# Attention beside a mixer MLP on one core: nine of sixteen key blocks in two 16-bit parts, and VectorE's background work in two classes

## The chip, the core and the metric

The kernel runs on one core of a Trainium2 chip. TensorE multiplies matrices into PSUM, VectorE and ScalarE do elementwise work, GpSimd fills constants and starts a few transfers, and SyncE's queue starts most of the DMA transfers. Each engine works through its own instructions in order and meets the others through semaphores. The metric is device time in microseconds of one execution.

## The reference

With x of 2048 tokens by 640 channels, 32 heads of 20 channels, and 1536 hidden channels of the MLP:

```python
xn = _layernorm(x, axis=-1)
return x + _A_ref(xn, A_wqkv, A_wo) + _B_ref(xn, B_w1, B_b1, B_w2, B_b2)
# _A_ref(x, wqkv, wo): q, k, v of 32 heads from x @ wqkv
scores = jnp.einsum("bhqd,bhkd->bhqk", q, k) * (Dh ** -0.5)
p = _softmax(scores, axis=-1)
o = jnp.einsum("bhqk,bhkd->bhqd", p, v)      # then @ wo
# _B_ref: normalises once more, then
h = _gelu(jnp.einsum("bsd,df->bsf", y, w1) + b1)
return jnp.einsum("bsf,fd->bsd", h, w2) + b2
```

All of it is float32. The kernel reaches that with products of 16-bit parts (a high part and a remainder), or with TensorE's slower float32 products.

## The kernel before

**Up to about 240 us** x is normalised and transposed, q, k and v are computed, and the weights of the MLP are split into 16-bit parts. The values v stay in SBUF, one block of rows per 128 keys. `SPLIT` (L25) says in which form: for a split block (two of every four) as a high and a low float16 part, for a whole block as float32. `vproj_out` (L355) writes them; VectorE computes the low part of a split block (L361).

**The attention stage** runs from there to about 1310 us. It has 64 passes, each for a pair of heads `g`, half of the tokens `hf`, and 512 tokens of that half `cc`. A pass goes over 16 key blocks in four groups of four (`GRP`). For each key block `scores` (L578) multiplies keys by queries for both heads on TensorE (L584) and ScalarE takes the exponential (L586) into a tile `p` of 128 keys by 2 heads by 512 tokens, float32. There are seven tiles `p` and three PSUM slots for scores. The sums over the keys are taken in `pv` (L603), one group behind: when the scores of a group are all issued, `pv(prev)` multiplies the group before. Its output is one PSUM tile `o` of 128 rows in four quarters of 32 rows. Each product (L615) has 32 output rows and so takes a quarter of TensorE's columns. A head has two quarters: 0 and 1 for the first, 2 and 3 for the second; `opart` receives both, and they are added later.

- For a split block, the upper 16 bits of `p`, read as bfloat16, are multiplied by the high value part in one quarter and by the low value part in the other: four products of 512 tokens for two heads. The remainder `low = p - upper(p)` in float16, which `rest` (L593) computes on VectorE (L598), is multiplied by the high value part: one product per head, alternating between the head's quarters from block to block.
- For a whole block, `p` and the values are multiplied in float32, one product per head, again alternating between the quarters.

`low` has four buffers. `rest` is called for the first block of a group after the second block's scores, and for the others after the fourth block's, just ahead of `pv(prev)`.

**The fill.** Between these, TensorE is given the MLP: `layer1` (L777) and `layer2` (L811), in portions with costs, and after them the output projection (L872). In each group, after the second block's scores, a credit grows by `rate` = 1.235 us, and portions are drawn while there is credit (L943 to L951). Both use the single PSUM bank pool `psM`, so the next tile of products waits until VectorE has read the one before: `gelu` (L735) for `layer1`, `addup` (L755) for `layer2`.

**The background work** is a list of Python generators, `sides`, each of which issues some instructions and yields. `tick` (L526), called after every second key block, takes one step of every generator in the list:

```python
def tick():
    for it in list(sides):
        if next(it, self_end) is self_end:
            sides.remove(it)
```

In that list are: `gelu` (seven VectorE instructions and a tanh on ScalarE, over five steps), `addup`, the loads of keys and queries (`load_stack`), the preparation of the output weights (`prep_late`, L534), and `finishing` (L661). The last normalises heads that are done: `finish` (L666) loads the two partial sums of some heads and the sums of exponentials, takes reciprocals (L702 to L707), sends them out and loads them back spread over rows, and then does four VectorE instructions on each strip of 512 tokens: add, multiply, high part, remainder (L725 to L731). A strip ends in a store to `oscr`, which the projection reads. `UNITS` gives the pairs of heads taken together; there are 23 strips.

At the end, after the last pass, the projection runs from `oscr` on its own (some 70 us), with the last heads' normalisation beside it.

Of the kernel before, what the change touches and what calls it, by code (L numbers as in the profile page):

```python
# [12 lines left out]
ALU = mybir.AluOpType  # L13
# [8 lines left out]
VW = DH + 1  # L22
PAD = 32 - VW
VROW = H * VW + PAD
SPLIT = (1, 1, 0, 0) * (NKB // 4)  # L25
NPAIR = H // 2
EPS = 1e-5
TOP = 15.5
# [7 lines left out]
TAIL = 12  # L36
# [6 lines left out]
def mha_mlp_kernel(tc, x, wqkv, wo, w1, b1, w2, b2, out):  # L43
# [4 lines left out]
    with (  # L48
# [463 lines left out]
        with ExitStack() as scope:  # L512
# [4 lines left out]
            ptp = pool(name="pt", bufs=2 * GRP - 1)  # L517


            sides = []  # L520

            def begin(it):

                if next(it, self_end) is not self_end:
                    sides.append(it)

            def tick():
                for it in list(sides):
                    if next(it, self_end) is self_end:
                        sides.remove(it)  # L530

            self_end = object()

            def prep_late(tag, w, wv_, src, nk, slices, delay):  # L534
                nc.sync.dma_start(w, src)
                for _ in range(delay):
                    yield
                acc = sm.tile([P, 8], F32, tag="acc", name="acc")
                for i, sl in enumerate(slices):
                    junk = m1.tile([P, 2 * MC], F32, tag="u", name="junk").bitcast(BF16)[:, :D]  # L540
                    nc.scalar.activation(junk, w[:, sl, :], AF.Square, accum_out=acc[:, i : i + 1])
                    yield
                pw[tag] = pow2(acc[:, : len(slices)], tag)
                s = keep.tile([P, 1], F32, name=f"s_{tag}")
                nc.vector.tensor_scalar(s, pw[tag][1], 4096.0, None, ALU.mult)
                nc.vector.tensor_scalar(fo, pw["v"][0], 2.0**-22, pw[tag][0], ALU.mult, ALU.mult)
                yield
                for k in range(nk):
                    parts = []
                    for tag_, c0 in (("u", 0), ("w", 320)):  # L550
                        tmp = m1.tile([P, 2 * MC], F32, tag=tag_, name="wtmp")[:, :320]
                        nc.vector.tensor_scalar(tmp, w[:, k, c0 : c0 + 320], s, None, ALU.mult)
                        parts.append((tmp, slice(c0, c0 + 320)))
                    yield
                    for tmp, cols in parts:
                        nc.vector.tensor_copy(wv_[:, k, 0, cols], tmp)
                        nc.vector.tensor_sub(wv_[:, k, 1, cols], tmp, wv_[:, k, 0, cols])
                    yield

            def project(ot, acc, t0, j):  # L560
                for hf in range(2):
# [41 lines left out]
            def pv(units):  # L603

                g, hf, cc, kb0 = units[0][:4]
                if kb0 == 0:
                    pv.o = psO.tile([P, 512], F32, tag="o", name="o")  # L610
                    pv.begun = set()
                last = units[-1][3] == NKB - 1

                def product(q, src, v0, t):
                    nc.tensor.matmul(pv.o[32 * q : 32 * q + 32, :], src[:, v0 - PAD * (1 - q % 2) :][:, :32], t,  # L615
                                     start=q not in pv.begun, stop=last, skip_group_check=True)
                    pv.begun.add(q)

                split = [(u[3], upper(u[4]), u[5]) for u in units if SPLIT[u[3]]]
                whole = [(u[3], u[4]) for u in units if not SPLIT[u[3]]]  # L620
                of16 = lambda kb, a: 2 * PAD + kb * 2 * VROW + (2 * g + a) * 2 * VW
                of32 = lambda kb, a: PAD + kb * VROW + (2 * g + a) * VW
                for kb, up, _ in split:
                    for a in range(2):
                        product(2 * a, vhalf, of16(kb, a), up[:, a])
                        product(2 * a + 1, vhalf, of16(kb, a) + VW, up[:, a])
                for a in range(2):
                    for n, (kb, _, low) in enumerate(split):
                        product(2 * a + n % 2, vhalf, of16(kb, a), low[:, a])
                for a in range(2):  # L630
                    for n, (kb, pt) in enumerate(whole):
                        product(2 * a + n % 2, vfull, of32(kb, a), pt[:, a])
                if last:
                    if cc == 0:
                        evs[g, hf] = m1.tile([P, 2, 512], F32, tag="ev", name="ev")
                    nc.scalar.activation(evs[g, hf][:, cc], pv.o, AF.Copy)  # L636
                    if cc == 1:
                        unload(g, hf, evs.pop((g, hf)))
# [5 lines left out]
            def unload(g, hf, ev):  # L644
                cols = slice(hf * 1024, (hf + 1) * 1024)
                for p in range(2):
                    dma(g, hf)(lpart[p, hf, 2 * g : 2 * g + 2, :].rearrange("a (c t) -> a c t", c=2),
                                      ev[PAD + DH + VW * p :: 64])
                    for a in range(2):
                        q0, r = 64 * a + PAD + VW * p, (2 * g + a) * DH  # L650
                        dma(g, hf)(opart[p, r : r + DH, cols].rearrange("d (c t) -> d c t", c=2),
                                          ev[q0 : q0 + DH])
                if g + 1 in ENDS:
                    fins.append(finish(g + 1 - UNITS[ENDS.index(g + 1)], g + 1, hf))
                    if len(fins) == 1:
                        sides.append(finishing())

            fins = []
            ready = [0, 0]
# [6 lines left out]
            def finish(g0, g1, hf):  # L666
# [9 lines left out]
                for c0 in range(0, 1024, w):  # L676
# [21 lines left out]
                    if c0 == 0:  # L698
                        for _ in range(W1 if last else 4):
# [3 lines left out]

                        nc.vector.tensor_scalar(l[:, 1], l[:, 0], LO, None, ALU.is_ge, ALU.min,
                                                accum_out=good[: nh * 16, n : n + 1])
                        nc.vector.tensor_scalar(l[:, 0], l[:, 0], 1e-30, None, ALU.max)
                        nc.vector.reciprocal(l[:, 1], l[:, 0])  # L707
                        if not last:
# [26 lines left out]
            def gelu(ps, r2f, hT, f):  # L735
                u = m1.tile([P, 2, MC], F32, tag="u", name="u")
                w = m1.tile([P, 2, MC], F32, tag="w", name="w")
                if f == 0:
                    nc.vector.tensor_scalar(r2f, r2f, f1, None, ALU.mult)
                nc.vector.tensor_mul(u, ps, r2f[:, None, :].to_broadcast([P, 2, MC]))  # L740
                nc.vector.tensor_add(u, u, b1t[:, f : f + 2, None].to_broadcast([P, 2, MC]))  # L741
                yield

                nc.vector.tensor_mul(w, u, u)  # L744
                nc.vector.scalar_tensor_tensor(w, w, 1.0 / 0.044715, u, ALU.add, ALU.mult)  # L745
                yield
                yield
                nc.scalar.activation(w, w, AF.Tanh, scale=0.7978845608028654 * 0.044715)
                yield
# [1 line left out]
                nc.vector.tensor_scalar(hT[:, f : f + 2, 0, :], u, ch, None, ALU.mult)  # L751
                nc.vector.scalar_tensor_tensor(hT[:, f : f + 2, 1, :], u, ch, hT[:, f : f + 2, 0, :],  # L752
                                               ALU.mult, ALU.subtract)

            def addup(ps, xb, t0, hf):  # L755
                cols = slice(hf * 320, (hf + 1) * 320)
                nc.vector.scalar_tensor_tensor(xb[:, cols], ps[:, :320], f2, xb[:, cols], ALU.mult, ALU.add)  # L757
                if hf == 1:
                    yield
                    nc.sync.dma_start(accscr[t0 : t0 + P, :], xb)  # L760
                    if t0 + P < S:
                        load_xb(t0 + P)
# [1 line left out]
            NMC = S // MC  # L764

            xs, hTs = {}, {}
            over = [False]

            def load_chunk(mc):
# [3 lines left out]
                nc.sync.dma_start(xnt, xscr[:, :, :, t0 : t0 + MC])  # L773
                nc.sync.dma_start(r2f, rscr[None, t0 : t0 + MC].to_broadcast([P, MC]))
                xs[mc] = xnt, r2f

            def layer1(mc, f):  # L777
                xnt, r2f = xs[mc]
# [91 lines left out]
            W1, W2 = 24, 17  # L870

            def projection():  # L872
                known = lambda c: ready[2 * c // NMC] == len(UNITS)
                for c in range(NMC):
                    while not known(c):
                        yield None
# [50 lines left out]
            with tc.manual_schedule():  # L927
# [2 lines left out]
                rate = 1.235  # L930
                groups = [(g, hf, cc, kb) for g, hf in ORDER for cc in range(2) for kb in range(0, NKB, GRP)]
                prev = None
                for g, hf, cc, kb0 in groups:
                    units = []
                    for kb in range(kb0, kb0 + GRP):
# [4 lines left out]
                        if kb % GRP == 1:  # L940
# [2 lines left out]

                            rest(units[0])
                            credit += rate
                            spent, over[0] = 0.0, False
                            while credit > 0 and spent < CHUNK and not over[0]:
                                cost = next(fill)
                                if cost is None:
                                    credit = 0.0  # L950
                                    break  # L951
                                credit -= cost
                                spent += cost
                        else:
                            for u in units[1:]:
                                rest(u)
                            if prev:
                                pv(prev)
                    prev = units
                    if cc == 0 and kb0 == 0 and (g, hf) != ORDER[-1]:  # L960
                        n = ORDER[ORDER.index((g, hf)) + 1]
# [16 lines left out]
                pv(prev)  # L978
                while more(1):
                    pass  # L980
                while sides:
                    tick()
                flag = nc.values_load(badi, min_val=0, max_val=1)
        with tc.If(flag > 0):
# [98 lines left out]
```

## Time and profile before

| | |
|---|---|
| median of 3 runs | 1384.71 us (1384.6 to 1388.05) |
| profiled execution | 1385.2 us, span 1383.5 us |
| TensorE products busy | 1350.8 us, 98% of the span |
| ScalarE busy | 1126.2 us, 81%; exponentials 973.6 us, x1024 |
| VectorE busy | 1061.7 us, 77%; `low` 608.8 us, x512 |
| gelu on VectorE | 7 instructions of 0.49 to 0.75 us, x48 |
| strips of head normalisation on VectorE | 4 instructions of 0.43 to 0.71 us, x23 |
| granted TensorE clock | 0.997 |
| HBM traffic | 123.7 MB, 89 GB/s over the span |

A row of the groups gives line, engine, operation, output and inputs, shapes and count, then busy time and mean duration of one, then the idle time of the engine just before these instructions and what ended it. TensorE's instructions overlap, four quarters above all, so their mean durations are longer than the distance from one to the next. In a row of stretches, each engine's busy time stands with its number of instructions; the last numbers are the granted clock, the busy share of the DMA engines and GB/s. A row of waits says who waited for whom, for how long in all, how often, and the longest.

### The profile page before, as it was taken

The page shows a single profiled execution, that of the slowest core. Times are in us where ns is not written, and L with a number is a line of the kernel's source. Part 1 is how long each engine was busy: PE and PEld are TensorE (multiplying, and loading weights), DVE is VectorE, ACT ScalarE, POOL GpSimd, SP SyncE. Part 2 cuts the span into 40 slices and gives each one's busy share as a digit, 9 for nine tenths or more (in the row PEclk, how much of TensorE's full clock was granted, in tenths as well). Part 3 has the DMA queues.
Part 4 walks back from the last instruction along what each step waited for, and adds up shares of the span by engine and source line. Part 5 has one row for each costly group of instructions (what it writes and reads, how often), then busy time and mean ns, then how long its engine had stood idle before and what let it go on. Part 6 is the DMA issues. An engine that isn't in the chain of part 4 may idle for free.

```text
span 1383.5 us, 29113 instructions
## 1 busy us (share of the span) xinstructions
PE 1350.8 (98%) x11711; PEld 600.9 (43%) x11711; DVE 1061.7 (77%) x1425; ACT 1126.2 (81%) x1282; POOL 32.9 (2%) x75
## 2 busy tenths in 40 slices
PE   9999999999999999999999999999999999999998
PEld 6555555443333343433343333343334334333375
DVE  6648743899778977889887789877988897888642
ACT  5644323999999999999999999999999999999700
POOL 2000000000000000000000000000000000000000
PEclk9999999999999999999999999999999999999999
DMA  9853413012124231213221123212124322341375
GB/s 265 243 175 109 108 52 110 16 32 64 41 55 111 67 88 34 69 52 102 71 77 33 47 75 103 76 47 58 44 64 113 98 56 70 85 153 59 98 235 179
DMA packets 92320, 125.68 MB, mean 91 GB/s; under 512 B 16905, under 2 KB 58569, under 8 KB 92178
## 3 DMA queue, kind: packets, MB, share of 16 engines
q1 hardware_dynamic: 89218, 117.14, 28.3%
q0 software_dynamic: 2304, 5.24, 2.3%
q8 instruction: 94, 1.54, 0.5%
q10 hardware_dynamic: 656, 1.36, 0.3%
q14 instruction: 48, 0.39, 0.1%
HBM read 80.84 MB, written 42.86 MB: 89 GB/s over the span
## 4 chain that ended last, share of the span: by engine, by line
PE 59%; DVE 11%; ACT 5%; DMA 3%; issue 2%; SPq 1%; DVEq 0%; ACTq 0%
PE o L615 23%; PE s L584 14%; PE py L819 9%; PE pu L787 8%; DVE low L598 5%; PE z L896 5%; ACT p L586 4%; DMA oscr<-oa 1%; DVE u L740 1%; DMA oa<-opart 1%; DVE u L741 1%; DVE w L744 1%; DVE w L745 1%; DVE hT L752 1%; DVE u L750 1%
## 5 line engine op out<-in xcount | busy, mean ns | idle before, releaser
L586 ACT ACTIVATE p<-s 128x1024 f32<-128x1024 f32 x1024 | 973.6, 1042 | 52.4 <-PE s L584 46.2
L598 DVE TENSOR_TENSOR low<-p 128x1024 f16<-128x1024 f32 x512 | 608.8, 1219 | 165.0 <-ACT p L586 164.9
L615 PE MATMUL o<-p,vfull 128*32 128x512 bf16 (+1 forms) x4096 | 433.7, 494 | 0.0
L584 PE MATMUL s<-qs,ks 61*128 61x512 f16 x2048 | 317.7, 382 | 8.7 <-ACT p L586 7.2
L584 PEld LDWEIGHTS <-ks 61*128 61x128 f16 x2048 | 63.9, 94 | 296.4 <-issue 294.2
L787 PE MATMUL pu<-xm,w1t 128*128 128x256 f16 x1440 | 179.2, 274 | 4.1 <-DVE u L740 3.6
L819 PE MATMUL py<-w2t,hT 128*128 128x320 f16 x1152 | 178.6, 301 | 1.7 <-DVE xb L757 1.7
L787 PEld LDWEIGHTS <-w1t 128*128 128x128 f16 x1440 | 130.9, 98 | 71.2 <-issue 57.6
L819 PEld LDWEIGHTS <-hT 128*128 128x128 f16 x1152 | 102.5, 98 | 89.5 <-issue 55.2
L286 PE MATMUL qkp<-xnt,wv 128*128 128x512 f16 x600 | 132.3, 380 | 0.0
L615 PEld LDWEIGHTS <-vfull 128*32 128x32 f16 x3072 | 61.5, 95 | 146.2 <-issue 115.4
L615 PE MATMUL o<-low,vfull 128*32 128x512 f16 x1024 | 107.3, 379 | 6.6 <-DVE low L598 6.4
L300 ACT ACTIVATE qkhl<-qkp,qks 128x1024 f16<-128x1024 f32 (+1 forms) x24 | 23.3, 971 | 84.1 <-PE qkp L286 66.2
L286 PEld LDWEIGHTS <-wv 128*128 128x128 f16 x600 | 58.2, 98 | 67.8
L615 PEld LDWEIGHTS o<-p,vfull 128*32 128x32 f32 x2048 | 63.1, 109 | 50.6 <-issue 0.5
L349 PE MATMUL vp<-wv,xnt 128*128 128x320 f16 x480 | 66.6, 300 | 0.0
L896 PE MATMUL z<-w1t,ot 128*128 128x320 f16 x480 | 65.8, 300 | 0.0
L896 PEld LDWEIGHTS <-ot 128*128 128x128 f16 x480 | 46.7, 98 | 19.8 <-issue 1.7
L349 PEld LDWEIGHTS <-xnt 128*128 128x128 f16 x480 | 46.5, 98 | 18.2
L301 DVE SCALAR_TENSOR_TENSOR qkhl<-qkp,qks,qkhl 128x1024 f16<-128x1024 f32 (+1 forms) x24 | 26.5, 1104 | 34.3 <-ACT qkhl L300 34.3
L857 DVE SCALAR_TENSOR_TENSOR acc<-z,sc,acc 128x320 f32<-128x320 f32 x32 | 17.6, 550 | 45.1 <-PE z L896 42.9
L636 ACT ACTIVATE ev<-o 128x512 f32<-128x512 f32 x64 | 39.4, 615 | 3.3 <-PE o L615 3.3
(168 smaller groups left out, 685.7 us busy)
## 6 DMA issues: line engine op xcount, KB each, us to landing
qkscr<-qkhl SPq DMA_DIRECT2D x40, 256.0 KB
opart<-ev SPq DMA_DIRECT2D x124, 80.0 KB
ks<-qkscr SPq DMA_DIRECT2D x120, 80.0 KB
qs<-qkscr SPq DMA_DIRECT2D x192, 40.0 KB
oa<-opart SPq DMA_DIRECT2D x32, 240.0 KB
xt<-in_A_x_dram SPq DMA_DIRECT2D x16, 320.0 KB
xscr<-xnt SPq DMA_DIRECT2D x4, 1280.0 KB
xm<-xscr SPq DMA_DIRECT2D x8, 640.0 KB
```

Source lines behind the costliest of these rows:

```text
L286: nc.tensor.matmul(ps[:, i, :], wv[:, k, q, a, mm * P : (mm + 1) * P], xnts[c][:, k, b, :], start=(k + n == 0), stop=(k == KD - 1 and n == 2))
L300: nc.scalar.activation(hl[:, 0, i0:i1], ps[:, i0:i1], AF.Copy, scale=a)
L301: nc.vector.scalar_tensor_tensor(hl[:, 1, i0:i1], ps[:, i0:i1], a, hl[:, 0, i0:i1], ALU.mult, ALU.subtract)
L349: nc.tensor.matmul(ps[:, hf, :320], xnts[c][:, k, a, j * P : (j + 1) * P], wv[:, k, 2, b, hf * 320 : (hf + 1) * 320], start=(n == 0), stop ...
L584: nc.tensor.matmul(ps[:, a, :], ks[64 * a : 64 * a + 61, kb * P : (kb + 1) * P], qs[64 * a : 64 * a + 61, cc * 512 : (cc + 1) * 512], star ...
L586: nc.scalar.activation(pt, ps, AF.Exp, scale=QS)
L598: nc.vector.tensor_sub(low, pt, upper(pt))
L615: nc.tensor.matmul(pv.o[32 * q : 32 * q + 32, :], src[:, v0 - PAD * (1 - q % 2) :][:, :32], t, start=q not in pv.begun, stop=last, skip_gr ...
L636: nc.scalar.activation(evs[g, hf][:, cc], pv.o, AF.Copy)
L787: nc.tensor.matmul(ps[:, i], w1v[:, k, (f + i) // 4, a, fo_ : fo_ + P], xnt[:, k, b, :], start=(n == 0), stop=(n == 3 * KD - 1))
L819: nc.tensor.matmul(ps[:, :320], hTs[mc][:, f, a, j * P : (j + 1) * P], w2v[:, f, b, hf * 320 : (hf + 1) * 320], start=(n == 0), stop=(n == ...
L896: nc.tensor.matmul(ps[:, :320], ot[:, k, a, j * P : (j + 1) * P], wov[:, k, b, h * 320 : (h + 1) * 320], start=(n == 0), stop=(n == 3 * KD ...
```

## The change

1. `SPLIT` becomes `(1, 1, 1, 0)` for the first four key blocks and stays `(1, 1, 0, 0)` for the others: nine split blocks of 16.
2. In the group with three split blocks and one whole block, the lower products of the third block and the float32 products of the whole one have no partner for the other quarter. `spread` gives such an odd block to both quarters of the head, 256 tokens to each.
3. `tick` has two classes. Generators now yield an estimate of the VectorE time that they issued. `sides` are stepped as before; those in `patient` only if nothing in `sides` issued timed work in that tick. `finishing` becomes patient, but for the last heads. `scale_ahead`, new and patient, multiplies a chunk's `r2f` by its factor before the chunk's first `gelu` needs it.
4. `prep_late` yields after each column half and waits two steps before its scale; the projection also waits for its end (`split_done`). `finish` has one more step in its reciprocals. `gelu` and `addup` yield costs.
5. In the first group of all, which has no `pv(prev)`, a portion of the fill is drawn at that point (`other`).

The numbers of buffers (four `low`, seven `p`, three score slots), the rate and the order of passes stay as they are.

```diff
-SPLIT = (1, 1, 0, 0) * (NKB // 4)
+SPLIT = (1, 1, 1, 0) + (1, 1, 0, 0) * 3
...
             def tick():
-                for it in list(sides):
-                    if next(it, self_end) is self_end:
-                        sides.remove(it)
+                t, taken[0] = taken[0], 0.0
+                for its in (sides, patient):
+                    if its is patient and t > 0:
+                        break
+                    for it in list(its):
+                        r = next(it, self_end)
+                        if r is self_end:
+                            its.remove(it)
+                        else:
+                            t += r or 0.0
...
-                def product(q, src, v0, t):
-                    nc.tensor.matmul(pv.o[32 * q : 32 * q + 32, :], src[:, v0 - PAD * (1 - q % 2) :][:, :32], t,
-                                     start=q not in pv.begun, stop=last, skip_group_check=True)
+                def product(q, src, v0, t, c0=0, c1=512):
+                    nc.tensor.matmul(pv.o[32 * q : 32 * q + 32, c0:c1], src[:, v0 - PAD * (1 - q % 2) :][:, :32],
+                                     t[:, c0:c1], start=q not in pv.begun, stop=last, skip_group_check=True)
                     pv.begun.add(q)
+
+                def spread(a, src, of, ts):
+
+                    for n, (kb, t) in enumerate(ts):
+                        if n % 2 == 0 and n + 1 == len(ts):
+                            for i in range(2):
+                                product(2 * a + i, src, of(kb, a), t[:, a], 256 * i, 256 * i + 256)
+                        else:
+                            product(2 * a + n % 2, src, of(kb, a), t[:, a])
...
                 for a in range(2):
-                    for n, (kb, _, low) in enumerate(split):
-                        product(2 * a + n % 2, vhalf, of16(kb, a), low[:, a])
+                    spread(a, vhalf, of16, [(kb, low) for kb, _, low in split])
                 for a in range(2):
-                    for n, (kb, pt) in enumerate(whole):
-                        product(2 * a + n % 2, vfull, of32(kb, a), pt[:, a])
+                    spread(a, vfull, of32, whole)
...
-                        sides.append(finishing())
+
+                        (sides if hf == 1 and g + 1 >= TAIL else patient).append(finishing())
...
-                if f == 0:
-                    nc.vector.tensor_scalar(r2f, r2f, f1, None, ALU.mult)
+                scale_rows(r2f)
...
+            def scale_rows(r2f):
+
+                if r2f in unscaled:
+                    unscaled.remove(r2f)
+                    nc.vector.tensor_scalar(r2f, r2f, f1, None, ALU.mult)
+
+            def scale_ahead(r2f):
+                for _ in range(8):
+                    yield
+                scale_rows(r2f)
...
-                known = lambda c: ready[2 * c // NMC] == len(UNITS)
+                known = lambda c: split_done and ready[2 * c // NMC] == len(UNITS)
...
                             for u in units[1:]:
                                 rest(u)
                             if prev:
                                 pv(prev)
+                            else:
+
+                                credit += rate
+                                other()
```

More of the change, by code (lines that the diff above doesn't have):

```diff
@@ L517, in mha_mlp_kernel @@
             ptp = pool(name="pt", bufs=2 * GRP - 1)
-            sides = []
+            sides, patient = [], []
+            taken = [0.0]
             def begin(it):
-                if next(it, self_end) is not self_end:
+                t = next(it, self_end)
+                if t is not self_end:
                     sides.append(it)
+                    taken[0] += t or 0.0
             def tick():
-                for it in list(sides):
-                    if next(it, self_end) is self_end:
-                        sides.remove(it)
+                t, taken[0] = taken[0], 0.0
[8 more added lines that the diff above has]
+                            t += r or 0.0
             self_end = object()
+            split_done = []
             def prep_late(tag, w, wv_, src, nk, slices, delay):
@@ L542, in prep_late @@
                     yield
+                yield
+                yield
                 pw[tag] = pow2(acc[:, : len(slices)], tag)
@@ L546, in prep_late @@
                 nc.vector.tensor_scalar(fo, pw["v"][0], 2.0**-22, pw[tag][0], ALU.mult, ALU.mult)
-                yield
+                yield 1.0
                 for k in range(nk):
@@ L553, in prep_late @@
                         parts.append((tmp, slice(c0, c0 + 320)))
-                    yield
+                    yield 0.6
                     for tmp, cols in parts:
@@ L557, in prep_late @@
                         nc.vector.tensor_sub(wv_[:, k, 1, cols], tmp, wv_[:, k, 0, cols])
-                    yield
+                        yield 0.7
+                split_done.append(tag)
             def project(ot, acc, t0, j):
@@ L705, in finish @@
                                                 accum_out=good[: nh * 16, n : n + 1])
+                        if not last:
+                            yield
                         nc.vector.tensor_scalar(l[:, 0], l[:, 0], 1e-30, None, ALU.max)
@@ L737, in gelu @@
                 w = m1.tile([P, 2, MC], F32, tag="w", name="w")
-                if f == 0:
-                    nc.vector.tensor_scalar(r2f, r2f, f1, None, ALU.mult)
+                scale_rows(r2f)
                 nc.vector.tensor_mul(u, ps, r2f[:, None, :].to_broadcast([P, 2, MC]))
                 nc.vector.tensor_add(u, u, b1t[:, f : f + 2, None].to_broadcast([P, 2, MC]))
-                yield
+                yield 1.2
                 nc.vector.tensor_mul(w, u, u)
                 nc.vector.scalar_tensor_tensor(w, w, 1.0 / 0.044715, u, ALU.add, ALU.mult)
-                yield
+                yield 1.2
                 yield
@@ L753, in gelu @@
                                                ALU.mult, ALU.subtract)
+                yield 1.7
+            def scale_rows(r2f):
[4 more added lines that the diff above has]
+                for _ in range(8):
+                    yield
+                scale_rows(r2f)
             def addup(ps, xb, t0, hf):
@@ L757, in addup @@
                 nc.vector.scalar_tensor_tensor(xb[:, cols], ps[:, :320], f2, xb[:, cols], ALU.mult, ALU.add)
-                if hf == 1:
-                    yield
+                if hf == 0:
+                    yield 0.5
+                else:
+                    yield 0.5
                     nc.sync.dma_start(accscr[t0 : t0 + P, :], xb)
@@ L766, in mha_mlp_kernel @@
             xs, hTs = {}, {}
+            unscaled = []
             over = [False]
@@ L775, in load_chunk @@
                 xs[mc] = xnt, r2f
+                unscaled.append(r2f)
+                if mc > 1:
+                    patient.append(scale_ahead(r2f))
             def layer1(mc, f):
@@ L932, in mha_mlp_kernel, with other @@
                 prev = None
+                def other():
+                    nonlocal credit
+                    spent, over[0] = 0.0, False
+                    while credit > 0 and spent < CHUNK and not over[0]:
+                        cost = next(fill)
+                        if cost is None:
+                            credit = 0.0
+                            break
+                        credit -= cost
+                        spent += cost
                 for g, hf, cc, kb0 in groups:
@@ L945, in mha_mlp_kernel @@
                             credit += rate
[L946 to L953, printed above, removed]
+                            other()
                         else:
@@ L958, in mha_mlp_kernel @@
                                 pv(prev)
+                            else:
+                                credit += rate
+                                other()
                     prev = units
@@ L980, in mha_mlp_kernel @@
                     pass
-                while sides:
+                while sides or patient:
                     tick()
```

## The prediction

> **What bounds the kernel now.** I read the page's busy times and slices first, to find the long stage and who is full in it, then busy times by stretches, the groups, the waits, and last the timeline of one group of key blocks. Engines and slices:
>
> ```profile
> PE 1350.8 (98%) x11711; PEld 600.9 (43%) x11711; DVE 1061.7 (77%) x1425; ACT 1126.2 (81%) x1282; POOL 32.9 (2%) x75
> DVE  6648743899778977889887789877988897888642
> ACT  5644323999999999999999999999999999999700
> ```
>
> From slice 8 to 38 the kernel is in attention, and there three engines are nearly full: VectorE's 77% is an average with the quiet ends. Stretches of that stage (span, then busy us of TensorE, weight loads, VectorE, ScalarE, GpSimd):
>
> ```profile
> 474.00:571.00 97.00, 96.55 (x900) 38.07 (x893) 75.72 (x81) 92.74 (x104) 1.27 (x2) 1.00 0.21 60
> 835.00:874.00 39.00, 36.25 (x339) 14.56 (x336) 37.90 (x51) 35.12 (x41) 0.00 (x0) 1.00 0.29 86
> 1255.00:1296.00 41.00, 36.75 (x328) 13.66 (x327) 36.88 (x65) 35.81 (x43) 0.87 (x1) 1.00 0.21 59
> ```
>
> In a light stretch (474 to 571) TensorE is busy 99.5% and VectorE 78%: TensorE bounds. Around 850 VectorE is at 97% and TensorE falls to 93%: VectorE bounds. The groups that the change touches (whole run, then 400 to 1200 us with forms apart):
>
> ```profile
> L598 DVE TENSOR_TENSOR low<-p 128x1024 f16<-128x1024 f32 x512 | 608.8, 1219 | 165.0 <-ACT p L586 164.9
> L615 PE MATMUL o<-p,vfull 128*32 128x512 f32 x1536 | 201.6, 592 | 0.0
> L615 PE MATMUL o<-p,vfull 128*32 128x512 bf16 x1536 | 122.7, 395 | 0.0
> L615 PE MATMUL o<-low,vfull 128*32 128x512 f16 x768 | 79.8, 378 | 3.9 <-DVE low L598 3.7
> ```
>
> One `low` costs VectorE 608.8/512 = 1.19 us. The waits between the engines look small:
>
> ```profile
> DVE low L598 <- ACT p L586: 164.9, 128, 8.2
> ACT p L586 <- PE s L584: 46.2, 132, 2.1
> PE o L615 <- DVE low L598: 6.4, 11, 1.5
> ```
>
> The last row understates: it counts from modelled ends. From start to start, the same stall is 23 places and 13.4 us; products of the MLP that wait for VectorE to empty their bank add 8 places and 5.8 us (after 250 us). So TensorE loses 19.2 us to VectorE. Scores that wait for ScalarE's slot add 45 places, 15 us. One group of four key blocks, and one with the stall:
>
> ```profile
> 700.04 0.64 PE L615 MATMUL o<-p,vfull 128*32 128x512 bf16 x8
> 700.50 0.39 PE L615 MATMUL o<-low,vfull 128*32 128x512 f16 x4
> 700.72 1.03 PE L615 MATMUL o<-p,vfull 128*32 128x512 f32 x8
> 701.68 0.39 PE L584 MATMUL s<-qs,ks 61*128 61x512 f16 x2
> ...
> 729.19 3.49 DVE L598 TENSOR_TENSOR low<-p 128x1024 f16<-128x1024 f32 x3
> 729.33 0.38 PE L615 MATMUL o<-low,vfull 128*32 128x512 f16 x1
> 730.46 0.40 PE L615 MATMUL o<-low,vfull 128*32 128x512 f16 x3 [0.76 <-DVE low L598]
> ```
>
> A group takes TensorE 1.64 us: 0.46 for upper parts, 0.22 for lower, 0.96 for whole blocks (two streams of records 0.43 apart, and 0.11 of change to the scores). At 730 the second lower product waits 1.1 us for VectorE, and all behind it on TensorE waits too.
>
> **TensorE's part.** Each of 64 passes (head pair, 512 tokens) turns one group from 2 split + 2 whole blocks into 3 + 1. Upper: one more round, +0.233 (half of 0.466). Lower: one round of half products; the 256-column `pu` products start 0.109 us apart, 512-column ones 0.216, so a half is half: +0.11. Whole: all four quarters work on 256 instead of 512 tokens, -0.427. Together -0.084 us, times 64 = -5.4 us. If a half cost as much as a whole, the group would be 0.45 us longer (+29 us); the 0.109 row is the nearest, and I keep -5.4. It counts only where TensorE bounds: 36 passes (below), -3.0 us; ScalarE, 95% busy in the light stretch, takes back about a third: -2.0.
>
> This needs that the first lower products of quarters 2 and 3 pass the halves still queued for 0 and 1. The fp32 row shows such passing: its eight records are four products of two records each, and all take 1.03 us, which is 0.43 + 0.59; so the first record of quarter 3 ran ahead of the second of quarter 0. The Trainium skill ("TensorE: Matmul & The Clock Gate", Part 3, "The mechanism") says the opposite: products are strict first in, first out, with no reordering, and only weight loads are pulled ahead. By that rule the odd group costs 0.215 us more, and the sum is that of the last rival; this row speaks against it.
>
> **VectorE's part.** 64 more `low` of 1.19 us: +76 us in the stage. To see where they fall I took the order in which the built programs give VectorE its work, and put the mean of each group's row on each instruction (a gelu 4.68 us, a strip of head normalisation 2.55, a sum 0.55), pass by pass, the last left out as it runs into the tail. A pass lasts 16.8 us (62 from 251 to 1292 us), or 16.2 without the 34 us of TensorE's waits. Before: 9.5 to 19.9 us per pass, mean 14.7; 20 passes over 16.2, by 32.7 us in all; 32 passes have more than 1 us to spare. After: 11.2 to 21.9, mean 15.9; 27 over, by 48.8 us; 22 with more than 1 us to spare. In this the yielding of the normalisation, the finer yields of the output weights' preparation and the earlier scaling of `r2f` (0.35 us) are contained: they only move work. Of 32.7 us of overload 19.2 became TensorE waits, 59%. At that share, 48.8 gives 28.6: +9.4; if all the growth becomes wait, +16.1. I take +13, nearer the upper end, since the light passes that swallowed the rest are fewer. Below it could be negative, down to -12.3: so much of the 19.2 us had normalisation among VectorE's work of the 8 us before. Passes that newly wait lose their waits for ScalarE (15/64 = 0.24 us each, some 13 passes): -3.
>
> Queues: `low` has four buffers, and now 3 + 2 live at once, so one `low` each of the odd group and the next waits for TensorE to read an older one. Behind it on VectorE stand gelu and sums. Between 0 and 1.2 us per pass (0 to 77 us); I take 0, as in full passes VectorE is behind TensorE anyway, and light ones have that much to spare. Between -1 and +3 go: the ninth value block's split (0.82 us, in the first 240 us, where VectorE is busy 60%); loads and stores of normalised heads, which go to SP's queue up to two passes later (the projection that reads them starts at the end); GpSimd's queue, which the moves leave alone; the first group's additional MLP work. That last takes 12 `z` products of 0.135 us (1.6 us) out of the tail, but `xm` lands only at 237.0 us, where the first `pu` waits now; asked for earlier, it holds up two scores on TensorE instead. I take 0, between -1.6 and +1.5.
>
> **Sum.** Profiled execution 1385.2 us (span 1383.5 and 1.7 around): -2.0 + 13 - 3 = +8, so 1393.2; it stands 0.5 above the median of the runs, 1384.7, so 1392.5 there.
>
> **Rivals.**
> *The cover holds, faster.* If VectorE's waits do not grow, because the normalisation leaves the crowded stretches: 1384.7 - 5.4 + 1.8 - 4 (a third of 12.3) = 1377; at the best 1369. It decides when the waits grow by less than 1 us. For it: 12.3 of 19.2 us stood near normalisation. Against: in the first 12 passes there is none, and there alone the overload goes from 4.6 to 8.9 us; the mean of 15.9 leaves 2%.
> *In between, no change.* Growth of 1 to 9 us of waits cancels against the TensorE gain: 1381 to 1388.
> *Quarters served in order, slower.* 36 passes gain nothing and lose 0.215 - 0.084 us instead of -0.084, so +7.7 on the forecast: 1400. Against: the fp32 row.
>
> **How the numbers follow.** Forecast 0.55 (own range 1389 to 1404); in order 0.07; no change 0.14; cover holds 0.24. About 0.3% (4 us) is what a measurement of this kernel can tell from no change. Faster 0.24, same 0.14, slower 0.62. The range leaves out the best fifth of the faster case and the worst of the slower ones: 1376 to 1405.
>
> **What would show it.** TensorE: in odd groups upper 0.70, lower 0.32, whole to next score 0.54 us; quarters 2 and 3 starting their lower products within 0.02 us of 0 and 1 if passing holds, 0.2 later if not. VectorE: busy about 1138 us, `low` x576; the waits of `o` for `low` doubled or more, most in passes with two gelus or a strip; the light stretch shorter, the crowded ones longer. Wrong if those waits stay near 13 us, or if `low` shows idle time for TensorE's reads of more than a few us.

## The result and the profile after

The changed kernel takes 1393.67 us (median of 6 runs, 1391.84 to 1395.11) against 1385.78 us for the kernel before (6 runs): a ratio of 1.0056, 95% interval 1.0046 to 1.0066, so slower by 0.6%, clear of the noise. The profiled execution took 1393.27 us, span 1391.6. The prediction was 1392.5, slower.

The groups of the page after, answering those shown of before (the line numbers moved: `low` is L614, the products of `pv` are L631, scores L600, exponentials L602):

```profile
PE 1351.9 (97%) x12223; PEld 618.4 (44%) x12223; DVE 1131.4 (81%) x1490; ACT 1129.1 (81%) x1282; POOL 32.9 (2%) x76
DVE  6658743999788988889998889997988998898732
...
L614 DVE TENSOR_TENSOR low<-p 128x1024 f16<-128x1024 f32 x576 | 682.6, 1218 | 107.2 <-ACT p L602 94.6
L631 PE MATMUL o<-p,vfull 128*32 128x512 bf16 (+2 forms) x4352 | 423.4, 462 | 0.0
```

VectorE's busy time grows by 69.7 us, and the idle time ahead of its `low` shrinks from 165.0 to 107.2 us: most of the additional work went into idle time, not all. The waits after:

```profile
DVE low L614 <- ACT p L602: 94.6, 90, 8.2
ACT p L602 <- PE s L600: 47.2, 120, 1.6
DVE low L614 <- PE o L631: 11.5, 12, 2.4
PE o L631 <- DVE low L614: 9.1, 20, 0.9
```

The third row is new: VectorE waits for TensorE to read an older remainder. The last one grew, but as before it understates, so I count the stalls from start to start: a group's time from its first upper product to the next scores, over its undisturbed 1.64 us (1.56 in the odd group), wherever it is more than 0.06 over ("remainder waits", 13.8 us before by this count); and the time by which the MLP's next tile starts late ("bank waits").

The same stretches as before, light and crowded (span, then busy us of TensorE, weight loads, VectorE, ScalarE, GpSimd; the kernel after):

```profile
474.00:571.00 97.00, 95.72 (x943) 39.41 (x932) 85.47 (x97) 92.25 (x104) 0.87 (x1) 1.00 0.26 71
835.00:874.00 39.00, 36.31 (x352) 14.95 (x350) 36.71 (x45) 34.66 (x40) 0.30 (x1) 1.00 0.28 77
```

In the light one VectorE went from 75.7 to 85.5 of 97 us, and TensorE's busy time fell there too (96.55 to 95.72); in the crowded one it hardly moved (36.25 to 36.31). Fixed times hold slightly different work in the two kernels, so here are whole passes, from first upper product to first upper product: the six that begin with the light stretch (at 477.7 us before) took 98.8 us before and 99.9 after, the two around 850 us 36.0 and 36.7.

An odd group that nothing disturbs, then one that waits (timeline of the kernel after: start, length, then as in the groups):

```profile
412.11 0.86 PE L631 MATMUL o<-p,vfull 128*32 128x512 bf16 x12
412.80 0.49 PE L631 MATMUL o<-low,vfull 128*32 128x512 f16 x8
413.12 0.60 PE L631 MATMUL o<-p,vfull 128*32 128x256 f32 x8
413.66 0.60 PE L600 MATMUL s<-qs,ks 61*128 61x512 f16 x4
...
730.94 0.87 PE L631 MATMUL o<-p,vfull 128*32 128x512 bf16 x12
731.27 2.35 DVE L614 TENSOR_TENSOR low<-p 128x1024 f16<-128x1024 f32 x2
731.63 0.38 PE L631 MATMUL o<-low,vfull 128*32 128x512 f16 x1
732.54 0.38 PE L631 MATMUL o<-low,vfull 128*32 128x512 f16 x1 [0.53 <-DVE low L614]
733.68 0.40 PE L631 MATMUL o<-low,vfull 128*32 128x256 f16 x4 [0.76 <-DVE low L614]
```

The first takes 1.55 us: 0.69 for upper parts, 0.32 for lower, 0.54 for the whole block. In the second TensorE stands at the second remainder, then at the third, 1.1 us after it: that third one is the subtraction that the change adds, and TensorE's queue holds everything behind it.

| attention stage | before | after | difference |
|---|---|---|---|
| remainder waits, us (places) | 13.8 (24) | 23.5 (38) | +9.8 |
| bank waits, us (places) | 5.8 (7) | 8.7 (12) | +2.9 |
| scores waiting for ScalarE's slot, from 250 us on, us | 12.9 | 11.6 | -1.3 |
| start of the first score to start of the last product, us | 1076.6 | 1084.6 | +8.1 |
| start of the last product to end, us | 74.5 | 74.2 | -0.3 |

The very first group of the stage is left out of the remainder waits: the granted clock is 0.50 there (237.8 to 241.2 us before). Of the 23.5 us, 13.8 stand in the odd groups, 19 places of the 64.

### The profile page after: what moved, and what is told of

Read it like the earlier page. It is cut to its first block, busy times and chain, and to the rows that moved or that the text cites. A ratio compares the mean times of both kernels' runs of the same rounds, so it can differ in the third digit from the quotient of the medians.

```text
span 1391.6 us, 30281 instructions
## 1 busy us (share of the span) xinstructions
PE 1351.9 (97%) x12223; PEld 618.4 (44%) x12223; DVE 1131.4 (81%) x1490; ACT 1129.1 (81%) x1282; POOL 32.9 (2%) x76
## 4 chain that ended last, share of the span: by engine, by line
PE 60%; DVE 13%; ACT 3%; issue 3%; DMA 2%; SPq 0%; DVEq 0%; ACTq 0%
PE o L631 23%; PE s L600 15%; PE py L862 10%; PE pu L830 8%; DVE low L614 7%; PE z L939 4%; ACT p L602 3%; DVE u L766 1%; DVE u L765 1%; DVE w L769 1%; DMA ks<-qkscr 1%; DMA oscr<-oa 0%; DVE hT L777 0%; DVE u L775 0%; DVE w L770 0%
## 5 line engine op out<-in xcount | busy, mean ns | idle before, releaser
L602 ACT ACTIVATE p<-s 128x1024 f32<-128x1024 f32 x1024 | 975.2, 1040 | 57.2 <-PE s L600 47.2
L614 DVE TENSOR_TENSOR low<-p 128x1024 f16<-128x1024 f32 x576 | 682.6, 1218 | 107.2 <-ACT p L602 94.6
L631 PE MATMUL o<-p,vfull 128*32 128x512 bf16 (+2 forms) x4352 | 423.4, 462 | 0.0
L600 PE MATMUL s<-qs,ks 61*128 61x512 f16 x2048 | 316.9, 382 | 7.2 <-ACT p L602 5.6
L600 PEld LDWEIGHTS <-ks 61*128 61x128 f16 x2048 | 64.0, 94 | 266.9 <-issue 264.3
L631 PEld LDWEIGHTS <-vfull 128*32 128x32 f16 x3584 | 76.8, 95 | 168.2 <-issue 121.8
L631 PE MATMUL o<-low,vfull 128*32 128x512 f16 (+1 forms) x1280 | 120.7, 357 | 9.8 <-DVE low L614 9.1
L631 PEld LDWEIGHTS o<-p,vfull 128*32 128x32 f32 x2048 | 65.8, 108 | 41.9
```

Of the source, the lines that this page charges most:

```text
L600: nc.tensor.matmul(ps[:, a, :], ks[64 * a : 64 * a + 61, kb * P : (kb + 1) * P], qs[64 * a : 64 * a + 61, cc * 512 : (cc + 1) * 512], star ...
L602: nc.scalar.activation(pt, ps, AF.Exp, scale=QS)
L614: nc.vector.tensor_sub(low, pt, upper(pt))
L631: nc.tensor.matmul(pv.o[32 * q : 32 * q + 32, c0:c1], src[:, v0 - PAD * (1 - q % 2) :][:, :32], t[:, c0:c1], start=q not in pv.begun, stop ...
```

## The experiments

Times are medians, with the ratio to the kernel before of the same chip session (1385.5 to 1386.0 us).

### The split alone

```diff
 # kernel before
-SPLIT = (1, 1, 0, 0) * (NKB // 4)
+SPLIT = (1, 1, 1, 0) + (1, 1, 0, 0) * 3
 # and product/spread as in the change; tick, finish, gelu, prep_late as before
```

> The kernel before with nine split blocks and the halves over both quarters, and nothing else of the change: background work steps as before. Theory load (64 more remainders on VectorE raise TensorE's waits for it from 19.6 to 32.2 us, against 5.4 us of shorter products): the waits are the same or larger, 32 to 38 us, and the time is 1394 to 1399 us. Rival steps (the finer and patient stepping of background work is what costs): the split alone gains its 5.4 us, 1380 to 1383 us.

1398.66 us, ratio 1.0093 (1.0077 to 1.0108). Remainder waits 28.0 us, bank waits 10.2. So the split costs 12.7 us by itself, in the old order of background work, and the stepping is not what makes the change slow.

### The stepping alone

```diff
 # changed kernel
-SPLIT = (1, 1, 1, 0) + (1, 1, 0, 0) * 3
+SPLIT = (1, 1, 0, 0) * (NKB // 4)
```

> The changed kernel with eight split blocks as before: only the stepping of background work, the earlier scaling and the additional portion in the first group are left of the change. Theory load: the order moves little, TensorE's waits for VectorE are 14 to 20 us, the time 1380 to 1386 us. Rival steps: the waits are near 32 us, the time 1391 us or more.

1377.89 us, ratio 0.9940 (0.9927 to 0.9954): faster than before by 8 us. Remainder waits 7.4 us, bank waits 3.3. The waits list of this run:

```profile
DVE low L614 <- ACT p L602: 160.5, 128, 8.2
PE o L631 <- DVE low L614: 3.7, 7, 0.8
```

So, taken in this order, the change is a gain of 8 us and a loss of 16 us (1377.9 to 1393.7) put together. The two parts do not simply add: taken the other way round, the split costs 12.7 us and the stepping then gives back 5.0 (1398.7 to 1393.7). That the order moves little was wrong: it took 9 us of waits away, not 0 to 6, and the time lies under the expected range.

### The split without its remainder

```diff
 # changed kernel, in rest()
+                if kb == 2:
+                    unit.append(rest.low)
-                if SPLIT[kb]:
-                    low = ptp.tile([P, 2, 512], F16, tag="low", name="low", bufs=GRP)
+                elif SPLIT[kb]:
+                    low = rest.low = ptp.tile([P, 2, 512], F16, tag="low", name="low", bufs=GRP)
```

> The changed kernel, but for the third key block no remainder is computed: its lower product takes the remainder of the second block, so 64 subtractions of VectorE are left out of the computation and TensorE's work is all there. Theory load: TensorE's waits for VectorE fall to those of before or under, 14 to 20 us, and the gain of the products shows: 1377 to 1382 us. Rival steps: the waits stay over 25 us and the time over 1388 us. Theory ring (four buffers for five live remainders make VectorE wait for TensorE) expects the same as load, since the fifth remainder is gone too.

1372.20 us, ratio 0.9903 (0.9888 to 0.9919), under the expected range, which did not know what the stepping is worth. Remainder waits 7.0 us, bank waits 3.7: the same as with the stepping alone. Between those two runs TensorE's products are the difference, and it is 5.7 us, where the sum of the prediction has 64 x 0.084 = 5.4. So with VectorE out of the way, the shorter products reach the end in full; the 64 subtractions cost 21.5 us (1372.2 to 1393.7), with the new stepping.

### The subtractions without the split

```diff
 # kernel before, in rest()
                     nc.vector.tensor_sub(low, pt, upper(pt))
                     unit.append(low)
+                elif kb == 2:
+                    idle = ptp.tile([P, 2, 512], F16, tag="idle", name="idle", bufs=1)
+                    nc.vector.tensor_sub(idle, pt, upper(pt))
 # the matrix of ones of pow2 moves to a shorter-lived pool, to make room
```

> The kernel before, with 64 additional subtractions on VectorE at the place of the third block's remainder, into a tile of their own that nobody reads; TensorE's work is unchanged, the four buffers are not touched. Theory load: 12 to 16 us more, 1397 to 1402 us, with TensorE's waits for VectorE at 32 to 38 us. Rival ring: without the pressure on the four buffers the additional work hides, 1386 to 1389 us.

1400.09 us, ratio 1.0106 (1.0090 to 1.0121). Nobody on TensorE reads this tile; the additional work only stands ahead of what TensorE needs. Remainder waits 23.1 us, bank waits 12.2. The load alone costs 14.1 us here, without the four buffers having a part. That is most of it and not all: the split alone, in the same stepping, costs 12.7 us net of 5.4 us of shorter products, so 18. There TensorE also waits for the third remainder itself (10.2 us of waits in the odd groups against 2.0 here).

### Five buffers

```diff
 # changed kernel
-                    low = ptp.tile([P, 2, 512], F16, tag="low", name="low", bufs=GRP)
+                    low = ptp.tile([P, 2, 512], F16, tag="low", name="low", bufs=GRP + 1)
 # the matrix of ones as above
```

> The changed kernel with five buffers for the remainders in place of four (room is made by keeping a constant matrix of ones in a shorter-lived pool). Rival ring: VectorE's 11.5 us of waiting for TensorE to read older remainders are what tips it; without them TensorE's waits fall to about 20 us and the time to 1380 to 1385 us. Theory load: VectorE has 97% of a pass to do either way, and its waits only let it start later in passes that have room; 1390 to 1394 us.

1393.10 us, against 1393.67 with four: no difference. VectorE's waits in this run:

```profile
DVE low L617 <- ACT p L605: 107.3, 90, 8.2
PE o L634 <- DVE low L617: 9.0, 20, 0.9
```

The row of VectorE waiting for TensorE is gone, and the wait for ScalarE's exponentials has grown from 94.6 to 107.3 us, by about the same. TensorE's remainder waits are 23.5 us, as before this edit. So the waits for the ring of four buffers fell into idle time that VectorE had anyway; without them it waits for the next exponentials instead.

### Whole products ahead of lower ones

```diff
 # changed kernel, in pv(); the kernel before likewise with its own two loops
-                for a in range(2):
-                    spread(a, vhalf, of16, [(kb, low) for kb, _, low in split])
                 for a in range(2):
                     spread(a, vfull, of32, whole)
+                for a in range(2):
+                    spread(a, vhalf, of16, [(kb, low) for kb, _, low in split])
```

In the changed kernel:

> The changed kernel with the float32 products of a group's whole blocks issued ahead of its lower products, so that the remainders are asked for 0.43 us later in the odd group and 0.85 us later in the others. Theory load, in which the cost is what the backlog of VectorE exceeds its lead by: of the 23.5 us of waits for remainders 7 to 14 stay, 1380 to 1387 us. If the backlog only grows on until it is met (VectorE short of time in whole passes, not in bursts), the time stays at 1391 to 1394 us.

1386.37 us, ratio 1.0005 (0.9996 to 1.0014): 7.3 us better than the changed kernel, level with the kernel before. The lead is the time that VectorE has before TensorE asks for its result. Remainder waits fall from 23.5 to 9.2 us, but bank waits rise from 8.7 to 15.5: half of what the longer lead saves is lost again at the next place where TensorE needs VectorE. The time lies in the range of the first expectation and not in that of the second: the backlog comes mostly in bursts that a longer lead covers, though part of it only moves to the next place. The waits of this run, at the next place and at the remainders:

```profile
PE pu L830 <- DVE u L765: 8.2, 8, 1.7
PE o L631 <- DVE low L614: 2.7, 6, 0.8
```

In the kernel before:

> The kernel before with the same exchange of whole and lower products. Theory load: of 13.8 us of waits for remainders 2 to 5 stay, the waits for the MLP's bank of 5.8 us stay or grow a little, 1375 to 1380 us. If the backlog only moves to the next place, 1384 to 1387 us.

1379.45 us, ratio 0.9955 (0.9941 to 0.9968), with remainder waits 3.6 and bank waits 8.0 us. With eight split blocks and the change's stepping:

> Eight split blocks, the change's stepping of background work, and whole products ahead of lower ones. Theory load: the 7.4 us of waits for remainders that the stepping alone left fall to 1 to 3 us, 1371 to 1375 us. If the backlog only moves on, 1376 to 1379 us.

1371.40 us, ratio 0.9901 (0.9886 to 0.9916). Remainder waits 0.7, bank waits 3.6 us. This is the best complete kernel of the study: 14 us under the kernel before and 22 under the changed one. In its list of waits TensorE's products for `o` have no row for `low` any more, and in its groups the products that read `low` have no idle time before them:

```profile
L614 DVE TENSOR_TENSOR low<-p 128x1024 f16<-128x1024 f32 x512 | 610.0, 1218 | 155.8 <-ACT p L602 155.3
L631 PE MATMUL o<-low,vfull 128*32 128x512 f16 x1024 | 100.9, 378 | 0.0
```

### The normalisation's giving way, taken back

```diff
 # the stepping alone (eight split blocks)
-                        (sides if hf == 1 and g + 1 >= TAIL else patient).append(finishing())
+                        sides.append(finishing())
```

> Eight split blocks and the change's other steps, but the normalisation of heads is stepped in every tick as before. If it is the normalisation's giving way that took 9 us of waits away, they come back: 1383 to 1386 us. If the finer steps of the output weights' preparation, the earlier scaling or the first group's portion did it, 1377 to 1380 us.

1381.54 us, ratio 0.9969 (0.9953 to 0.9985): between the two expectations. With the other steps in place, giving way is worth 3.7 us; the other steps without it are worth 4.3. Remainder waits are 11.7 us and bank waits 4.1 here. Which of the other steps has the 4.3 us was not separated. In the pass where the output weights are prepared the remainder waits are 0.4 us in this run against 2.0 before, which fits the finer steps of `prep_late`. The portion in the first group is a rival: in this trace it brings 2.8 us of `gelu` on VectorE into the first pass, which had none before, and moves later `gelu`s to other passes. Nor does giving way just undo waits of the kernel before: some 4.7 us of the waits of this run stand in two passes, from 642 and from 1042 us, where neither the kernel before nor the stepping alone has any.

### The third remainder on GpSimd

```diff
 # changed kernel with whole products first
-                    nc.vector.tensor_sub(low, pt, upper(pt))
+                    (nc.gpsimd if kb == 2 else nc.vector).tensor_sub(low, pt, upper(pt))
```

> The changed kernel with whole products ahead of lower ones, and the third block's remainder computed by GpSimd, which is busy 2% of the span, in place of VectorE. Theory load: VectorE is back at the work of eight split blocks; with the shorter products this gives the run with eight blocks and the same order, 1371.4 us, less some 5 us: 1365 to 1370 us, if GpSimd needs under 4 us for one and VectorE's own instructions keep their durations. Rival: the two engines get in each other's way or the third remainder comes too late, the remainders of VectorE last longer than 1.22 us or TensorE waits for GpSimd, and the time is over 1375 us.

1450.85 us, ratio 1.0458 (1.0435 to 1.0482). The rival holds. GpSimd needs 2.19 us (median) for one, well under 4, but it works through its queue in order too, and there stands the load that adds the bias to `xb`. Timeline of GpSimd, where an odd group's products began at 710.1 us:

```profile
714.50 0.86 POOL L852 DMA_DIRECT2D xb<-in_B_b_dram  x1 [21.36 <-DMA xb<-in_A_x_dram]
715.12 2.18 POOL L614 TENSOR_TENSOR low<-p 128x1024 f16<-128x1024 f32 x1
```

The remainder stands behind an issue that waits for `xb` to land, and TensorE waited 6.4 us in that group. Six such groups lost 33 us, the odd groups together 60. After each of these six waits the granted clock stands at half for 3.4 to 10.2 us, which it does nowhere else in this run between 250 us and the end of the stage. After the wait shown, and then:

```profile
715.60:722.40 6.80, 5.05 (x27) 1.70 (x30) 4.34 (x5) 2.52 (x3) 1.69 (x1) 0.50 0.28 48
722.40:735.00 12.60, 12.60 (x128) 5.55 (x124) 10.27 (x12) 11.62 (x14) 2.56 (x1) 1.00 0.10 29
```

TensorE is busy for 24 us in these six stretches; half of that, 12 us, is an estimate of what the clock costs. With the 50 us by which the waits for remainders exceed the 9.2 us of the same order on VectorE alone, this accounts for nearly all of the 64.5 us between the two runs. VectorE's remainders that overlap one of GpSimd's lasted 1.63 us in the mean (61 of them), the other 451 lasted 1.22. The Trainium skill ("GPSIMD Engine Reference", "Key points") says that the two share their SBUF interfaces and contend where VectorE's instruction has two SBUF inputs, which `low` has; this trace agrees.

## Why the prediction was right, point by point

**The TensorE term.** Predicted upper 0.70, lower 0.32, whole to next score 0.54 us; the medians are 0.690, 0.323 and 0.542, a group of 1.560 us against 1.645. The size, -5.4 us, is right to 0.3 us where VectorE leaves it alone (the run without the third remainder). But the sum took only -2.0 of it, on the argument that 36 passes would keep it and ScalarE take back a third; that was not tested by itself. The light stretch, which was to get shorter, did not.

**Quarters passing each other.** In the undisturbed odd group, by the recorded starts, quarters 2 and 3 begin their lower products 0.01 us after 0 and 1, though halves for 0 and 1 stand ahead of them in the program; eight products take 0.49 us in all. The rival of quarters served in order is out. The Trainium skill's rule of strict order ("TensorE: Matmul & The Clock Gate", Part 3, "The mechanism") does not hold here for products that wait for their own quarter. It does where the wait is for a semaphore: at 731.63 us one product starts, and those for the free quarters 2 and 3 wait behind the one that stands for VectorE.

**The VectorE term.** +13 us was predicted, and remainder and bank waits together went from 19.6 to 32.2, +12.6. But it was put together from other parts than I thought. I said of the stepping and the earlier scaling that "they only move work", inside the sum over the order. Measured, the stepping takes 9 us of waits away (19.6 to 10.7, with the split undone), and the subtractions add 21.5 (10.7 to 32.2). The sum over the order held both. Done again in the same way from the traces, VectorE's work over 16.2 us per pass adds up to 32.9 us before, 47.5 after, 22.5 with the stepping alone and 61.6 with the split alone; the prediction's 59% of the last two is 13 and 36 us of waits, and 10.7 and 38.2 were counted. So the way of reckoning saw both parts, and what was mis-sized is that sentence, and with it the price of the split: 16 us net beside the new stepping, not 8. The reckoning does not see the order within a pass: with the giving way taken back it gives 22.7 us, hardly more than with it, but the waits are 15.8. And +13, between +9.4 and +16.1, was a judgement.

**ScalarE's slots.** -3 us predicted, -1.3 measured from 250 us on. (In the first group before that, TensorE's wait for `xm` takes the place of two waits of scores.)

**The first group's portion and the queues.** Predicted 0, as `xm` lands at 237.0 us. In the trace after, the first `pu` waits for it:

```profile
237.32 0.86 PE L830 MATMUL pu<-xm,w1t 128*128 128x256 f16 x6 [2.45 <-DMA xm<-xscr]
```

and the last stretch is shorter by 0.3 us only, though 12 `z` products did move out of it. The account of the stage: -5.4 + 12.6 - 1.3, and 1.6 for these 12 products, are 7.5 of the 8.1 us by which it grew; 0.6 stay open.

**The total.** The prediction had -2.0, +13, -3 and 0 in these four places, together +8 (on 1384.7 that is 1392.7; the 1392.5 given is 0.2 off). The TensorE term in the sum was 3.4 us too small, and the terms of the slots and of the portion missed the other way by 1.7 and 1.6. That the total agrees within about a microsecond is in part luck. That the change is slower is not: it rests on the VectorE term, and the runs with the 64 subtractions alone and without them show it.

**The buffers.** The price of 0 was right: five buffers change nothing. The sign that I named for being wrong, idle time of VectorE for TensorE's reads of more than a few us, did appear (11.5 us) and was no sign: it was spare time under another name. One other sign came out smaller than named: the waits for remainders grew to 1.7 times (13.8 to 23.5 us), where doubled or more was named.

**The faster rival.** A gain of this kind is there: without the split, giving way is worth 3.7 us and the other steps 4.3. That it comes from the normalisation leaving crowded passes is not shown, as VectorE's work over 16.2 us per pass is nearly the same with it and without (22.5 and 22.7 us). The rival lost because the waits with 64 more subtractions grew all the same.

## What to carry to other kernels

Trading TensorE time for VectorE time is priced by the engine that has the least spare time in the crowded stretches, not by its mean: 5.7 us of products were bought with 21.5 us of waits while VectorE's busy share read 77%. A change of several parts should be taken apart before it is kept or dropped; here one part was worth 8 us by itself, and the other cost 13 by itself and 16 beside the first. And where an in-order engine must wait for another, the cheapest lead is to issue first what does not need the other: exchanging two loops gave 6 us in each of two versions of the kernel and 7 in a third.

## What was not expected of the hardware

Products for a quarter of TensorE's columns pass others that wait for their own quarter (they start 0.01 us after the first, ahead of halves that stand before them), and do not pass one that waits for a semaphore (1.1 us at one product in the group from 730.94 us). A remainder on GpSimd takes 2.19 us against VectorE's 1.22, and lengthens VectorE's own by a third while they overlap (1.63 against 1.22 us). After waits of 4.0 to 7.8 us on TensorE, the granted clock was at half for 3.4 to 10.2 us; after the waits of up to 2.0 us in the same run's odd groups it was not.
